# Threshold attention followed by a gMLP: half-batch loads shaped by GpSimd, and gMLP work two steps later

## The chip, the cores and the metric

One NeuronCore of a Trainium2 chip. The metric is device time in microseconds (us) of one execution. The kernel before took 701.15 us, the median of three runs (699.99 to 705.87). Engines are named as in the profile: PE is TensorE (PEld its weight loads), DVE VectorE, ACT ScalarE, POOL GpSimd, SP SyncE, whose queue (SPq) issues nearly all DMAs here. "Rounds" are repeated timings of a kernel beside the kernel before on the same chip.

## The reference, cut to what matters

Shapes: q, k, v are 8 batches x 8 heads x 576 x 64; the gMLP has 512 inputs and 1024 hidden columns.

```python
scores = scale * np.matmul(q, k.transpose(0, 1, 3, 2))
thresh = np.max(scores, axis=-1, keepdims=True) - tau          # tau = 0.02
scores = np.where(scores >= thresh, scores, -1e9)
attn = exp(scores - max); attn /= attn.sum(-1) + 1e-9
x = (attn @ v)  -> (B, S, H*D)
h = np.maximum(x @ w_in, 0);  u, v = h[..., :512], h[..., 512:]
v_n = (v - mean(v)) / np.sqrt(var(v) + 1e-6)                   # LayerNorm (LN)
v_s = w_spatial @ v_n + b_spatial
out = (u * v_s) @ w_out
```
(The middle lines are abridged.)

## The kernel before: the parts concerned

Thirty-two pairs of heads are walked as *slots*, each of five *steps* of query rows. A step makes scores on PE, their maxima on DVE (`negm`), exponentials on ACT (`e`), the thresholded product on DVE (`p`, "the mask"), and a transposing DMA (`pT`; `pTr` for the half-size fifth step). The scores of 64 key columns of each head are one product with `kd`, a small operand that Pool copies together. One or two filler products stand behind the scores: the transposes of the next pair's q and k (`qk_main`), the product with v (`pv`), or a piece of the gMLP (`moe_v`, `moe_u`, `moe_s`, `moe_o`).

```python
for slot in range(NPAIR + 5):
    i = slot if slot < NPAIR else None
    for c in range(5):
        fillers = []
        # ... qk_main(slot + 1, 0/1) at c = 0/1, qk_rem at c = 2; pv(slot - 1) at c = 3, 4
        if slot >= 5:
            b, ph = divmod(slot - 5, 4)
            fillers.append((moe_v, moe_u, moe_s, moe_o)[ph](b, c))
        step(i, c, fillers)
        if c == 3 and slot + 2 < NPAIR:
            load(slot + 2)          # q, k, v of one pair, q and k in runs of 256 B
```
When a pair's output is complete, it is transposed into `xT`, and a part of it moved by Pool:

```python
# end of pv, second head
nc.sync.dma_start_transpose(out=xts[b][:, hp, :]..., in_=xns[i]...)
nc.gpsimd.tensor_copy(out=xts[b][64:128, hp, 512:576], in_=xts[b][64:128, hp, 576:640])
```
Pool took its instructions in the order of this program.

Of the kernel before, what the change touches and what calls it, by code (L numbers as in the profile page):

```python
# [8 lines left out]
F32 = mybir.dt.float32  # L9
# [8 lines left out]
def kernel(  # L18
# [14 lines left out]

    nc = tc.nc
# [6 lines left out]
    P = 128  # L41
    const = ctx.enter_context(tc.tile_pool(name="const", bufs=1))
    ld = ctx.enter_context(tc.tile_pool(name="ld", bufs=2))
    qkT = ctx.enter_context(tc.tile_pool(name="qkT", bufs=2))
    ep = ctx.enter_context(tc.tile_pool(name="ep", bufs=3))
    ptp = ctx.enter_context(tc.tile_pool(name="ptp", bufs=10))
# [3 lines left out]
    xtp = ctx.enter_context(tc.tile_pool(name="xtp", bufs=3))  # L50
# [17 lines left out]
    pr_ring = [const.tile([P, 640], BF16, name=f"pr{i}") for i in range(2)]  # L68
    v_ring = [const.tile([P, 2, 6, D + 1], BF16, name=f"v{i}") for i in range(4)]
    vn_ring = [const.tile([P, 5, 512], BF16, name=f"vn{i}") for i in range(2)]  # L70
    kd_ring = [const.tile([P, P], F32, name=f"kd{i}") for i in range(2)]
    qd_ring = [const.tile([P, P], F32, name=f"qd{i}") for i in range(2)]
    for t in kd_ring + qd_ring:
        nc.gpsimd.memset(t, 0.0)
    for t in pr_ring:
        nc.gpsimd.memset(t[:, S:640], 0.0)
    for t in v_ring:
        nc.gpsimd.memset(t[:, :, :, D:D + 1], 1.0)
        nc.gpsimd.memset(t[64:128, 0, 4, :], 0.0)
        nc.gpsimd.memset(t[0:64, 1, 4, :], 0.0)  # L80
        nc.gpsimd.memset(t[64:128, 1, 5, :], 0.0)
# [7 lines left out]
    wsl = const.tile([P, 5, S], F32, name="wsl")  # L89
# [4 lines left out]


    loaded = {}

    def load(i):
        b, hp = divmod(i, HP)
        ts = []  # L100
        for nm, src in (("qn", q), ("kn", k)):
            t = ld.tile([P, 5, 2, D], F32, name=nm)
            for h in range(2):
                nc.sync.dma_start(  # L104
                    out=t[:, 0:4, h, :],
                    in_=src[b, 2 * hp + h, 0:512, :].rearrange("(p c) d -> p c d", c=4))
            nc.sync.dma_start(out=t[0:64, 4, :, :],  # L107
                              in_=src[b, 2 * hp:2 * hp + 2, 512:576, :].rearrange("h p d -> p h d"))
            ts.append(t.rearrange("p c h d -> p c (h d)"))
        t = ld.tile([P, 2, 5, D], F32, name="vl")  # L110
        s2 = v[b, 2 * hp:2 * hp + 2]
        nc.sync.dma_start(
            out=t[:, :, 0:4, :],
            in_=s2[:, 0:512, :].rearrange("h (p c) d -> p h c d", c=4))
        nc.sync.dma_start(out=t[0:64, :, 4, :],
                          in_=s2[:, 512:576, :].rearrange("h p d -> p h d"))
        nc.sync.dma_start(out=t[64:128, 1, 4, :], in_=s2[1, 512:576, :])
        ts.append(t)
        loaded[i] = ts
        vt = v_ring[i % 4]  # L120
        nc.gpsimd.tensor_copy(out=vt[:, :, 0:4, 0:D], in_=ts[2][:, :, 0:4, :])  # L121
        nc.gpsimd.tensor_copy(out=vt[0:64, 0, 4, 0:D], in_=ts[2][0:64, 0, 4, :])
        nc.gpsimd.tensor_copy(out=vt[0:64, 1, 5, 0:D], in_=ts[2][0:64, 1, 4, :])
        nc.gpsimd.tensor_copy(out=vt[64:128, 1, 4, 0:D], in_=ts[2][64:128, 1, 4, :])


    def load_weights():
        nc.gpsimd.dma_start(out=w_in, in_=moe_w_in.rearrange("(f p) n -> p f n", p=P))
        nc.gpsimd.dma_start(out=w_o, in_=moe_w_out.rearrange("(f p) n -> p f n", p=P))
        nc.sync.dma_start(out=wsl[:, 0:4, :],  # L130
                          in_=moe_w_spatial[0:512, :].rearrange("(p c) s -> p c s", c=4))
        nc.sync.dma_start(out=wsl[0:64, 4, :], in_=moe_w_spatial[512:576, :])
        brow = const.tile([1, S], F32, name="brow")
        nc.sync.dma_start(
            out=brow[0:1, 0:512].rearrange("o (c p) -> o c p", c=4),
            in_=moe_b_spatial[0:512].rearrange("(o p c) -> o c p", o=1, c=4))
        nc.sync.dma_start(out=brow[0:1, 512:576],
# [3 lines left out]
        for c in range(5):  # L141
            n = P if c < 4 else 64
            nc.gpsimd.tensor_copy(
                out=wsb[:n, c, 0:512].rearrange("p (sc sp) -> p sc sp", sc=4),
                in_=wsl[:n, c, 0:512].rearrange("p (sp sc) -> p sc sp", sc=4))
            nc.gpsimd.tensor_copy(out=wsb[:n, c, 512:576], in_=wsl[:n, c, 512:576])
        for c in range(5):
            nc.sync.dma_start_transpose(out=wsT[:, :, c * P:(c + 1) * P], in_=wsb[:, c, :])
# [15 lines left out]
    qts, kts, rems, pts, xns, xts = {}, {}, {}, {}, {}, {}  # L164

    def qk_main(i, which):
        src = loaded[i][which]
        dst = qkT.tile([P, 512], F32, name="qT" if which == 0 else "kT")
        (qts if which == 0 else kts)[i] = dst
        hold = {}  # L170

        def mm():
            t = ps_f.tile([P, 512], F32, name="f")
            hold["t"] = t
            for c in range(4):
                nc.tensor.transpose(out=t[:, c * P:(c + 1) * P], in_=src[:, c, :],  # L176
                                    identity=identf)

        def ev():
            nc.scalar.activation(out=dst, in_=hold["t"], func=ACT.Copy,  # L180
                                 scale=scale if which == 0 else 1.0)
        return mm, ev

    def qk_rem(i):
        hold = {}

        def mm():
            t = ps_f.tile([P, 512], F32, name="f")
            hold["t"] = t
            for w in range(2):  # L190
                nc.tensor.transpose(out=t[:, w * 64:w * 64 + 64],
                                    in_=loaded[i][w][0:64, 4, :],
                                    identity=identf[0:64, 0:64])

        def ev():
            rem = qkT.tile([P, P], F32, name="rem")
            rems[i] = rem
            nc.scalar.copy(out=rem, in_=hold["t"][:, 0:P])
            for lo in (0, 64):
                hs = slice(lo, lo + 64)  # L200
                nc.gpsimd.tensor_scalar(out=qd_ring[i % 2][hs, hs], in0=rem[hs, 0:64],
                                        scalar1=scale, scalar2=0.0, op0=ALU.mult, op1=ALU.add)
                nc.gpsimd.tensor_copy(out=kd_ring[i % 2][hs, hs], in_=rem[hs, 64:128])  # L203
        return mm, ev

    def pv(i, h):
# [4 lines left out]
        def mm():  # L211
            t = ps_f.tile([P, 512], F32, name="f")
            hold["t"] = t
            for c in range(5):
                for ki in range(5):
                    blk = ki if (c == 4 or h == 0 or ki == 4) else 5 + ki
                    vb = 5 if (c == 4 and h == 1 and ki == 4) else ki
                    nc.tensor.matmul(out=t[:, c * 65:c * 65 + 65], lhsT=pts[i, c][:, blk, :],  # L218
                                     rhs=vt[:, h, vb, :], start=(ki == 0), stop=(ki == 4))
# [17 lines left out]
        return mm, ev  # L237

    vns, us, gs = {}, {}, {}

    def moe_v(b, c):
# [9 lines left out]
        def ev():  # L251
            vrel = vr.tile([P, 512], F32, name="vrel")
            nc.scalar.activation(out=vrel, in_=hold["t"], func=ACT.Relu)  # L253
            st = small.tile([P, 6], F32, name="st")
            nc.vector.bn_stats(out=st, in_=vrel)  # L255
            mv = small.tile([P, 2], F32, name="mv")
            nc.vector.bn_aggr(out=mv, in_=st)
            rs = small.tile([P, 1], F32, name="rs")
            nc.gpsimd.tensor_scalar(out=rs, in0=mv[:, 1:2], scalar1=1e-6, scalar2=1.0,
                                    op0=ALU.add, op1=ALU.mult)  # L260
            nc.gpsimd.tensor_tensor(out=rs, in0=rs, in1=mhalf, op=ALU.pow)
            nm = small.tile([P, 1], F32, name="nm")
            nc.gpsimd.tensor_scalar(out=nm, in0=mv[:, 0:1], scalar1=rs, scalar2=-1.0,
                                    op0=ALU.mult, op1=ALU.mult)
            n = P if c < 4 else 64
            nc.gpsimd.tensor_scalar(out=vn_ring[b % 2][:n, c, :], in0=vrel[:n],  # L266
                                    scalar1=rs[:n], scalar2=nm[:n],
                                    op0=ALU.mult, op1=ALU.add)
        return mm, ev

    def cols(n):
        return (0, 512) if n == 0 else (512, 64)

    def moe_u(b, f):
# [17 lines left out]
        def ev():  # L292
# [3 lines left out]
            if f < 4:  # L296
# [5 lines left out]
        return mm, ev  # L302

    def moe_s(b, f):
# [28 lines left out]
        return mm, ev  # L333

    def moe_o(b, c):
# [10 lines left out]
        def ev():  # L346
            o = vr.tile([P, 512], F32, name="o")
            nc.scalar.copy(out=o[:n], in_=hold["t"][:n])
# [3 lines left out]
        return mm, ev  # L352


    pend_ev = []
    pend_mask = []

    def step(i, c, fillers):

        if i is not None:  # L360
            qT, kT = qts[i], kts[i]
            s = ps_s.tile([P, 1536], F32, name="s")
            A, Bh = slice(0, 64), slice(64, 128)
            if c < 4:
                cs = slice(c * P, (c + 1) * P)


                nc.tensor.matmul(out=s[:, 0:512], lhsT=qT[A, cs], rhs=kT[A, :],  # L368
                                 start=True, stop=True)
# [113 lines left out]
```

## Time and profile before

| | before |
|---|---|
| median | 701.15 us |
| busy: PE / DVE / ACT / POOL | 73 / 68 / 42 / 30% |
| PE waits for q's load | 52.0 us in 28 slots |
| PE waits for xT before moe_v | 41.2 us in 8 batches |
| first row maxima | 33.19 us after the start |

Busy shares alone say little here: no engine is full. The lines of the profile stand in the prediction, with their reading.

### The profile page before, as it was taken

Reading aid. Unit: us, or ns where it says so; the run is one execution under the profiler, and the core shown is the slowest. Engines: PE = TensorE matmul, PEld = TensorE weight load, DVE = VectorE, ACT = ScalarE, POOL = GpSimd, SP = SyncE. Lnnn points to the kernel's source line nnn. Section 1 sums busy time; section 2 is a strip of 40 time slices with the busy share of each in tenths; the row PEclk is TensorE's granted clock in tenths of the full one; section 3 lists DMA queues with packets and bytes.
Section 4 is the critical chain, followed back from the end, with each engine's and each line's share of the span. In section 5 each row is a group of like instructions: output and inputs, shape, how many; then the busy total and the mean of one; then the engine's idle time right before and its main releaser. Section 6 shows DMA issues by size and latency. Waiting matters only on the chain.

```text
span 704.7 us, 10528 instructions
## 1 busy us (share of the span) xinstructions
PE 517.9 (73%) x3712; PEld 265.5 (38%) x3712; DVE 479.0 (68%) x570; ACT 299.2 (42%) x506; POOL 209.1 (30%) x497
## 2 busy tenths in 40 slices
PE   2177775888856788578858888567896888588876
PEld 1034442444423444244424444234442444244432
DVE  0067776788837787487857888377864888578931
ACT  1044444364524544354443645245352554336332
POOL 5601112451214311344114511143112452145031
PEclk9977777899979999899988999899997999889999
DMA  6947877377956567468693779565575677838531
GB/s 169 145 101 134 147 134 155 54 141 141 179 125 115 114 121 172 102 121 139 127 197 62 144 139 182 122 110 116 107 176 112 113 141 140 195 64 139 97 103 67
DMA packets 297786, 90.94 MB, mean 129 GB/s; under 512 B 283718, under 2 KB 292422, under 8 KB 297606
## 3 DMA queue, kind: packets, MB, share of 16 engines
q1 hardware_dynamic: 296678, 88.71, 64.8%
q0 software_dynamic: 1056, 1.57, 1.4%
q8 instruction: 29, 0.48, 0.3%
q14 instruction: 23, 0.19, 0.1%
HBM read 33.31 MB, written 9.44 MB: 61 GB/s over the span
## 4 chain that ended last, share of the span: by engine, by line
PE 28%; DVE 22%; DMA 14%; SPq 11%; ACT 11%; issue 8%; POOL 5%; POOLq 0%; ACTq 0%; DVEq 0%
DVE negm L386 12%; PE s L368 10%; DMA qn<-in_q_dram 9%; ACT e L389 7%; DVE p L402 6%; SPq L104 5%; PE s L372 4%; DMA xT<-xn 3%; PE f L218 3%; PE f L176 3%; PE f L343 2%; PE f L282 2%; POOL vn L266 2%; SPq L406 2%; SPq L107 2%
## 5 line engine op out<-in xcount | busy, mean ns | idle before, releaser
L389 ACT ACTIVATE e<-s,negm 128x576 f32<-128x576 f32 x256 | 175.7, 738 | 284.0 <-DVE negm L386 284.0
L386 DVE TENSOR_REDUCE negm<-s 128x2 f32<-128x1152 f32 x128 | 172.8, 1350 | 114.2 <-PE s L372 113.6
L402 DVE SCALAR_TENSOR_TENSOR p<-e,ctau 128x1152 bf16<-128x1152 f32 x128 | 181.5, 1418 | 0.0
L368 PE MATMUL s<-kT,qT 64*128 64x512 f32 x256 | 163.3, 721 | 4.2 <-ACT e L389 3.8
L370 PE MATMUL s<-kT,qT 64*128 64x512 f32 x256 | 163.3, 721 | 0.0
L121 POOL CAST v<-vl 128x512 bf16<-128x512 f32 x32 | 19.8, 618 | 291.3 <-DMA vl<-in_v_dram 245.0
L372 PEld LDWEIGHTS s<-kd,qT 128*128 128x128 f32 x256 | 41.4, 203 | 133.2 <-issue 107.7
L372 PE MATMUL s<-kd,qT 128*128 128x128 f32 x256 | 67.4, 348 | 21.6 <-POOL kd L203 21.6
L248 PE MATMUL f<-w_in,xT 128*128 128x512 bf16 x160 | 48.8, 427 | 41.5 <-DMA xT<-xn 41.2
L255 DVE BATCH_NORM_STATS2 st<-vrel 128x6 f32<-128x512 f32 x40 | 27.7, 692 | 73.7 <-ACT vrel L253 73.5
L218 PE MATMUL f<-v,pT 128*128 128x65 bf16 x1280 | 51.1, 193 | 34.1 <-ACT vrel L253 12.9
L176 PE MATMUL f<-identf,qn 128*128 128x128 f32 x128 | 23.8, 317 | 59.0 <-DMA qn<-in_q_dram 52.0
L218 PEld LDWEIGHTS <-pT 128*128 128x128 bf16 x1280 | 49.6, 99 | 40.4 <-issue 34.3
L368 PEld LDWEIGHTS s<-kT,qT 64*128 64x128 f32 x256 | 42.9, 209 | 53.2 <-issue 36.9
L266 POOL TENSOR_SCALAR vn<-vrel,rs,nm 128x512 bf16<-128x512 f32 (+1 forms) x40 | 53.2, 1329 | 4.0
L253 ACT ACTIVATE vrel<-f 128x512 f32<-128x512 f32 x40 | 24.1, 602 | 46.4 <-PE f L248 43.3
L343 PE MATMUL f<-w_o,gT 128*128 128x512 bf16 (+1 forms) x160 | 41.4, 387 | 2.8 <-DVE xn L227 1.7
L370 PEld LDWEIGHTS s<-kT,qT 64*128 64x128 f32 x256 | 42.9, 209 | 0.0
L313 PE MATMUL f<-wsT,vn 128*128 128x512 bf16 x160 | 41.0, 390 | 2.3 <-POOL vn L266 1.4
L396 ACT ACTIVATE e<-s,negm 128x576 f32<-128x576 f32 x32 | 23.7, 741 | 40.6 <-DVE negm L393 40.6
L176 PEld LDWEIGHTS f<-identf,qn 128*128 128x128 f32 x128 | 15.9, 159 | 63.8 <-issue 63.8
L248 PEld LDWEIGHTS <-xT 128*128 128x128 bf16 x160 | 15.8, 108 | 59.1 <-DMA xT<-xn 45.5
(71 smaller groups left out, 633.0 us busy)
## 6 DMA issues: line engine op xcount, KB each, us to landing
qn<-in_q_dram SPq DMA_DIRECT2D x64, 128.0 KB, 2.9
kn<-in_k_dram SPq DMA_DIRECT2D x64, 128.0 KB, 2.8
vl<-in_v_dram SPq DMA_DIRECT2D x32, 256.0 KB, 3.0
out_dram<-o SPq DMA_DIRECT2D x32, 256.0 KB, 2.6
pT<-p SPq DMA_TRANSPOSE x128, 3.3
wsl<-in_moe_w_spatial_dram SPq DMA_DIRECT2D x1, 1152.0 KB, 6.1
qn<-in_q_dram SPq DMA_DIRECT2D x32, 32.0 KB, 2.5
kn<-in_k_dram SPq DMA_DIRECT2D x32, 32.0 KB, 2.4
```

What stands on the lines that cost most here:

```text
L176: nc.tensor.transpose(out=t[:, c * P:(c + 1) * P], in_=src[:, c, :], identity=identf)
L218: nc.tensor.matmul(out=t[:, c * 65:c * 65 + 65], lhsT=pts[i, c][:, blk, :], rhs=vt[:, h, vb, :], start=(ki == 0), stop=(ki == 4))
L248: nc.tensor.matmul(out=t, lhsT=xts[b][:, f, c * P:(c + 1) * P], rhs=w_in[:, f, 512:1024], start=(f == 0), stop=(f == 3))
L266: nc.gpsimd.tensor_scalar(out=vn_ring[b % 2][:n, c, :], in0=vrel[:n], scalar1=rs[:n], scalar2=nm[:n], op0=ALU.mult, op1=ALU.add)
L313: nc.tensor.matmul(out=t, lhsT=vn[:, c, f * P:(f + 1) * P], rhs=wsT[:, c, 0:512], start=(c == 0), stop=(c == 4))
L343: nc.tensor.matmul(out=t[:n], lhsT=gs[b][:, f, c * P:c * P + n], rhs=w_o[:, f, :], start=(f == 0), stop=(f == 3))
L368: nc.tensor.matmul(out=s[:, 0:512], lhsT=qT[A, cs], rhs=kT[A, :], start=True, stop=True)
L370: nc.tensor.matmul(out=s[:, 1024:1536], lhsT=qT[Bh, cs], rhs=kT[Bh, :], start=True, stop=True)
L372: nc.tensor.matmul(out=view(s, 512, [[448, 2], [1, 64]]), lhsT=qT[:, cs], rhs=kd_ring[i % 2], start=True, stop=True)
L386: nc.vector.tensor_reduce(out=nm, in_=both, axis=AX.X, op=ALU.max, negate=True)
L389: nc.scalar.activation(out=e[:, h, :], in_=both[:, h, :], func=ACT.Exp, bias=nm[:, h:h + 1])
L402: nc.vector.scalar_tensor_tensor(out=pt, in0=pe.rearrange("p h s -> p (h s)"), scalar=ctau, in1=pe.rearrange("p h s -> p (h s)"), op0=ALU. ...
```

## The change

Its intent: load two pairs at once in 1 KB runs, two slots ahead, so that PE never waits for q; let moe_v start two steps later (27 steps instead of 25), so that its xT has landed; make masks and transposes of the last step simpler; take LN's statistics from DVE to ACT; bring the weights in while slot 1 runs. The core of the diff:

```diff
+    def load_qk(i, n):                     # n = 2: both pairs of half a batch
+        ...
+            nc.sync.dma_start(
+                out=t[:, :, 0:4, :],
+                in_=src[:, 0:512, :].rearrange("h (p c) d -> p h (c d)", c=4))
+    def shape_qk(i):                       # Pool: head-interleaved copy for the transposes
+        ...
+            if w == 0:
+                nc.gpsimd.tensor_scalar(out=t, in0=src, scalar1=scale, ...)
+            else:
+                nc.gpsimd.tensor_copy(out=t, in_=src)
...
-            nc.vector.bn_stats(out=st, in_=vrel)
-            nc.vector.bn_aggr(out=mv, in_=st)
+            nc.scalar.activation(out=vrel, in_=hold["t"], func=ACT.Relu, accum_out=sm)
+            ...
+                nc.scalar.activation(out=sq, in_=vrel, func=ACT.Square, bias=nmean,
+                                     accum_out=ss)
...
-        for slot in range(NPAIR + 5):
+    LAG = 27
+        for g in range(20 * B + LAG):
+            slot, c = divmod(g, 5)
+            if c == 0 and i is not None:
+                if slot % 2 == 0 and slot + 2 < NPAIR:
+                    load_qk(slot + 2, 2)
+                    load_v(slot + 2)
+                if slot + 1 < NPAIR:
+                    shape_qk(slot + 1)
+                shape_v(slot)
+                if slot == 1:
+                    load_weights()
```
(The last batch has its own placement, with LN on DVE, uT evacuated by DVE and every other output copy on DVE; the last step's scores are four small products; its `pTr` is transposed in two halves. The lines are abridged, and `...` stands for what is left out.) The xT copy stays where it was, at the end of `pv`. In the program it now comes directly ahead of the next `shape_qk`.

## The prediction

> **What bounds the kernel now.** I read the page, then the list of waits, the timeline of some slots, and the gaps in TensorE's timeline. A *slot* is one pair of heads, five *steps* of 128 query rows (the fifth is half size). In each step TensorE makes the scores and one or two filler products, DVE takes row maxima (`negm`), ACT the exponentials, DVE masks (`p`), and the DMA transposes.
>
> ```profile
> PE 517.9 (73%) x3712; PEld 265.5 (38%) x3712; DVE 479.0 (68%) x570; ACT 299.2 (42%) x506; POOL 209.1 (30%) x497
> ...
> PEclk9977777899979999899988999899997999889999
> ...
> L386 DVE TENSOR_REDUCE negm<-s 128x2 f32<-128x1152 f32 x128 | 172.8, 1350 | 114.2 <-PE s L372 113.6
> ...
> L402 DVE SCALAR_TENSOR_TENSOR p<-e,ctau 128x1152 bf16<-128x1152 f32 x128 | 181.5, 1418 | 0.0
> ```
>
> No engine is full. DVE is next to TensorE, and a step costs it 1.35 + 1.42 = 2.77 us. What stretches a slot is in the waits:
>
> ```profile
> ACT e L389 <- DVE negm L386: 284.0, 128, 25.8
> ...
> PE f L176 <- DMA qn<-in_q_dram: 52.0, 28, 5.0
> ...
> PE f L248 <- DMA xT<-xn: 41.2, 8, 6.3
> ```
>
> The first is only ACT's spare time. The second is the start of nearly every slot: the next pair's q arrives late because its load is issued one step ahead. The third comes once per batch: the first gMLP product (moe_v) follows directly on the last head's output, whose transpose has not landed. The timeline shows both, with TensorE's cold clock after the longer one (a score pass of 1.22 us, otherwise 0.69):
>
> ```profile
> 309.11 0.63 PE L176 MATMUL f<-identf,qn 128*128 128x128 f32 x4 [1.20 <-DMA qn<-in_q_dram]
> ...
> 326.66 0.63 PE L176 MATMUL f<-identf,qn 128*128 128x128 f32 x4 [1.89 <-DMA qn<-in_q_dram]
> ...
> 366.19 1.35 SPq L406 DMA_TRANSPOSE pT<-p  x1
> ...
> 367.63 1.24 SPq L232 DMA_TRANSPOSE xT<-xn  x1
> ...
> 370.27 0.61 PE L248 MATMUL f<-w_in,xT 128*128 128x512 bf16 x1 [5.55 <-DMA xT<-xn]
> 370.28 0.24 POOL L235 COPY xT<-xT 64x64 bf16<-64x64 bf16 x1 [2.22 <-DMA xT<-xn]
> ...
> 370.81 1.22 PE L368 MATMUL s<-kT,qT 64*128 64x512 f32 x1
> ```
>
> I mark a slot by T, the start of its q transposes. T runs from 144.03 to 636.81 over six batches: 82.1 us a batch, 20.5 a slot; a moe_u slot is 17.55 (309.11 to 326.66), and the slot with moe_v has 27. Before that, the start: scores are ready at 11 us, but their correction operand `kd` stands on Pool behind the preparation of the weights:
>
> ```profile
> 8.51 0.26 ACT L198 COPY rem<-f 128x128 f32<-128x128 f32 x1
> ...
> 31.28 0.23 POOL L201 TENSOR_SCALAR qd<-rem 64x64 f32<-64x64 f32 x1
> ...
> 32.35 0.80 PE L372 MATMUL s<-kd,qT 128*128 128x128 f32 x2 [21.61 <-POOL kd L203]
> ```
>
> **What the Trainium skill says.** *TensorE: Matmul & The Clock Gate*, Part 1: an idle window of about 3.4 us halves the clock, and a similar busy time restores it. Agrees: each gap of 3.4 us or more in the before trace is followed by about 4 us of slow passes; several gaps of only 1.9 to 2.3 us are too. *GPSIMD Engine Reference*, Specifications: Pool shares its SBUF interfaces with VectorE and contends with DVE instructions with two SBUF inputs. Agrees; the mask is one, and a 0.26 us Pool operation that starts inside it ends with it:
>
> ```profile
> 319.78 1.41 DVE L402 SCALAR_TENSOR_TENSOR p<-e,ctau 128x1152 bf16<-128x1152 f32 x1
> ...
> 319.84 1.48 POOL L263 TENSOR_SCALAR nm<-mv,rs 128x1 f32<-128x1 f32 x1
> ```
>
> *DMA: Bandwidth & Descriptors*, Specifications: runs of 512 B and more are needed for line rate. Here q lands 128 KB in 256 B runs in 2.9 us and v 256 KB in 1 KB runs in 3.0 us: long runs carry more, but what is waited for is latency. *ScalarE: Activation LUTs*, What ACT_TABLE_LOAD costs: 280 ns + 0.833 ns per element with a pointer bias. The exponentials agree (0.74 us for 576).
>
> **The change part by part.**
>
> Loads. Two pairs are fetched together, two slots ahead: the wait for q's DMA (52 us, plus SP's issue time before it) goes. But Pool must now bring q and k into shape at the top of the slot in which TensorE transposes them. By the order of Pool's instructions in the changed build, each slot's q shaping stands directly *behind* the small xT copy (L235 before), which waits for the xT transpose of the step just ended. A new chain replaces the load: xn, SP, xT DMA, Pool copy, Pool shaping, q transpose. Shaping 640 elements I estimate at 0.92 us: Pool's unblocked tensor_scalar takes 0.77 for 512 and 0.19 for one element.
>
> The slot, walked from T = 0 in a moe_u slot. q transposes 0.5, filler 0.9 and scores 1.55 end at 2.95. From there DVE has: max 1.36, mask 1.41, max, mask (8.5), a gap of 0.35 for TensorE, max, mask (11.6), xn 0.7, short max 0.74, mask 1.41, xn 0.7: 15.15. SP issues the mask's transpose first (1.3 us from 14.5, to 15.8), xT lands 2.6 later (18.45), copy 0.3 (18.75), q shaping with hand-over 1.0: the next T is at 19.75. Before it was 17.55: 2.2 us lost. TensorE has finished the next slot's first scores at 14.9 and idles 4.85 us, longer than before's 1.2 to 1.9.
>
> The other three slots of a batch. With moe_s the output products are the first filler and xn comes before the mask, so xT starts at 14.85: 18.75 in all. The slot after it has two gT products left on DVE: 20.4. The slot in which moe_v starts has its LN work on Pool (rs, pow, nm, vn of three blocks, some 2.1 us each, stopped during masks) ahead of the xT copy: the walk gives 22.25; the next, with two more squares on ACT, 20.5. Sum 18.75 + 20.4 + 22.25 + 20.5 = 81.9 a batch with a warm clock. This already contains the gains: xT is now two steps ahead of moe_v (41 us of waiting off), bn_stats and bn_aggr leave DVE (35 us of 479, seven eighths of it), a Square of about 0.71 us (estimate from the ScalarE page) goes to ACT, which has room at 42%. So what is gained in the moe_v slots (27 to 22) is given back in the others: 81.9 against 82.1.
>
> The clock. Four gaps of 2.7 to 7 us per batch instead of one of 5.5 to 6 and some of 2. A cold start delays the filler and first scores by about 1.7 us (a score group ran 2.65 us instead of 1.5, the filler 1.41 instead of 1.03, cut off after 4 us). Three or four per batch: 5 to 6 us, up to 88 a batch. Over the 6.75 batches with gMLP: -1 to +40 us.
>
> Start. kd no longer waits for the weights: first maxima at about 14 instead of 33.19 us, 19 gained. But load_weights now runs in slot 1 through three buffers of the exponentials' ring, and SP holds its loads and transposes in turn: three loads of some 4 us, five blocks of casts at 1.3, five wsT issues at 1.3 to 2, then 4.6 us for the bias; SP frees the pending `pTr` at about 55. I find the T of slot 2 at 67, against 66.56 before. Slots 2 to 4 have the new chain as well (18 instead of 17): in all +5.
>
> The rest. Fifth step as four small products (about 1.3 us, as now), kd first: nothing. The split pTr adds one SP issue of 1.25 us a slot, not on the chain. Tail: two more steps, but LN partly on DVE and output copies on two engines: -2.
>
> Sum: 701 + 5 - 2 - 1 = 703 warm; 701 + 5 - 2 + 40 = 744 with every slot cold.
>
> **Rivals.** (1) The loads were the bound and shaping is hidden: slots near 18, DVE's 14.35 us plus 3 to 4. For it: DVE is contiguous in my walk and only the chain keeps the slot at 20; against it: Pool is in order and the copy's wait stands ahead. It would make 640 to 670. (2) DVE or ACT becomes the bound: DVE's total of about 455 us plus start and tail says no. (3) The weights' stall in slot 1 is much shorter, 40 instead of 67: 10 to 20 us off, 685 to 695. (4) Pool shaping slowed by masks or by strided reads, 1.5 to 2 us rather than 0.9: 30 us more, 735 to 770.
>
> **Range and chances.** The sum spans 703 to 744. The cold case agrees better with the gaps before, but the change is plainly tuned (a lag of 27, a last batch of its own), which makes me suspect that my serial walk overstates a hand-over somewhere; so I put the time at 718, below the middle. Range 680 to 750: rival 3 at the low end, the cold sum at the high. Faster by over 2% (under 687) needs rival 1 or 3: 0.22. Within 2%: 0.30. Slower: 0.48.
>
> **What would show it.** TensorE's q transposes should wait for Pool's qn (instead of DMA), 3 to 5 us in nearly every slot, and Pool's xT copy for the xT DMA just before; the wait of moe_v for xT should be gone; T to T about 20 in moe_u slots; score passes of 1.22 us at most slot starts, mean clock at or below 0.91; DVE near 455 us; the first maxima at 14 us and a hole between 30 and 60. If q transposes wait less than 1.5 us a slot, my chain is wrong and rival 1 holds.

## The result, and the profile after

The changed kernel took 755.5 us (median of 4 runs, 749.93 to 757.43), the kernel before 701.85 us beside it (4 runs, 699.99 to 705.87): ratio 1.074, 95% interval 1.068 to 1.081. A ratio is the mean time of one kernel's runs over that of the other's in the same rounds, so not quite the ratio of the medians quoted. The change was slower by 7%, and the time lies outside the predicted range. All outputs are right.

Busy times and the granted clock of the changed kernel (from the page; each digit is a fortieth of the span, in tenths of full speed):

```profile
PE 528.8 (71%) x3840; PEld 278.6 (37%) x3840; DVE 460.4 (62%) x516; ACT 324.6 (43%) x605; POOL 210.2 (28%) x427
PEclk9755987888988999988988999888998789989998
```
DVE fell from 479.0 to 460.4 us, as intended. PE's busy time grew by 11 us although its large products are the same (3840 instructions against 3712, since the fifth step's scores are now four small products): it ran colder, with a mean granted clock of 0.86 against 0.912. The same 128 q transposes, for one, took 33.2 us instead of 23.8.

The list of waits of the changed kernel (engine, who is waited for: us in total, times, longest):

```profile
POOL xT L261 <- DMA xT<-xn: 234.2, 25, 13.1
...
PEld f L208 <- POOL qn L142: 172.3, 30, 8.1
...
PE f L208 <- POOL qn L142: 147.8, 30, 7.3
```
The 52 us of waiting for q's DMA became 147.8 us of waiting for Pool to shape q, 4.9 us on average in 30 slots. The first line tells what Pool was doing: standing at the small copy until the xT transpose landed. The stall that the lag of 27 was meant for is gone: moe_v waited for xT once, 2.7 us, against 41.2 us in 8 batches.

One such slot start, from the timeline (start, duration, engine, instruction; in brackets the idle time before and who ended it):

```profile
427.28 0.49 DVE L253 TENSOR_TENSOR xn<-f,r 128x320 bf16<-128x320 f32 x1
...
428.60 1.25 SPq L258 DMA_TRANSPOSE xT<-xn  x1
...
431.31 0.23 POOL L261 COPY xT<-xT 64x64 bf16<-64x64 bf16 x1 [5.41 <-DMA xT<-xn]
...
431.63 0.72 POOL L142 TENSOR_SCALAR qn<-ql 128x640 f32<-128x640 f32 x1
...
432.41 1.12 PE L208 MATMUL f<-identf,qn 128*128 128x128 f32 x4 [4.29 <-POOL qn L142]
...
433.32 1.91 PE L324 MATMUL f<-xT,w_in 128*128 128x512 bf16 x4
```
Read it downwards: the output `xn` ends at 427.77, SP gets to its transpose 0.8 us later, Pool's copy starts at 431.31 when it has landed, only then does Pool shape q, for whose load it does not have to wait, and PE starts at 432.41. That is 4.64 us from `xn` to PE. The last line is the clock: the product of four takes 1.91 us where a warm one takes 1.04.

PE's q transposes at the start of four consecutive slots in the changed kernel:

```profile
237.40 1.11 PE L208 MATMUL f<-identf,qn 128*128 128x128 f32 x4 [7.27 <-POOL qn L142]
...
259.26 1.11 PE L208 MATMUL f<-identf,qn 128*128 128x128 f32 x4 [4.24 <-POOL qn L142]
...
279.37 0.65 PE L208 MATMUL f<-identf,qn 128*128 128x128 f32 x4 [2.52 <-POOL qn L142]
...
299.19 1.11 PE L208 MATMUL f<-identf,qn 128*128 128x128 f32 x4 [5.28 <-POOL qn L142]
```
Slots of 21.9, 20.1 and 19.8 us; the fourth ends at 322.52 (23.3 us): 85.1 us for the batch, where the kernel before needs 82.1 by the prediction's reading and 83.1 on average from pair 6 to pair 31.

Where the 43.3 us between the two profiled spans (704.7 to 748.0) arose follows from three marks on PE, the start of the q transposes T of pair 6 and of pair 31, and the end: pair 6 at 130.29 instead of 117.44 (+12.9, the start), pair 31 at 671.00 instead of 636.81 (34.2 late, so +21.3 in the loop), the end 43.3 late (+9.1 in the tail). The marks split the span, so they add up by construction. They do not cover everything: the profiled execution of the kernel before was a slow one of its kind (706.51 us) and that of the changed kernel its fastest (749.93), while the medians are 53.7 us apart. Where the other 10 us arise, these two traces do not tell.

The start of the changed kernel, where the weights come in (timeline):

```profile
13.53 1.36 DVE L460 TENSOR_REDUCE negm<-s 128x2 f32<-128x1152 f32 x1 [12.63 <-PE s L415]
...
34.23 0.54 SPq L170 DMA_DIRECT2D e<-in_moe_w_spatial_dram  x1
41.80 1.07 POOL L178 CAST wsb<-e 128x512 bf16<-128x512 f32 x1 [14.18 <-DMA e<-in_moe_w_spatial_dram]
...
44.28 1.37 ACT L468 ACTIVATE e<-s,negm 128x576 f32<-128x576 f32 x2 [16.02 <-POOL wsb L181]
...
63.99 1.25 SPq L443 DMA_TRANSPOSE pTr<-pr  x1
```
The maxima come at 13.5 us instead of 33.2, but then a piece of w_spatial, held in one of the three buffers of the exponentials, stops ACT for 16 us, SP with the transposes of `wsb` and the bias lets `pTr` go only at 64, and the 20 us gained are lost and more.

In the tail, LN's blocks of the last batch follow one another on DVE and Pool, hand by hand (timeline of the changed kernel; the last of five blocks, and the next product of u):

```profile
726.83 0.69 DVE L287 BATCH_NORM_STATS2 st<-vrel 128x6 f32<-128x512 f32 x1
727.55 0.18 DVE L289 BATCH_NORM_AGGREGATE mv<-st 128x2 f32<-128x6 f32 x1
727.77 0.15 DVE L290 TENSOR_SCALAR rs<-mv 128x1 f32<-128x1 f32 x1
728.00 0.55 POOL L292 TENSOR_TENSOR rs<-rs,mhalf 128x1 f32<-128x1 f32 x1 [1.67 <-DVE rs L290]
728.59 0.54 DVE L293 TENSOR_SCALAR vn<-vrel,mv,rs 64x512 bf16<-64x512 f32 x1 [0.66 <-POOL rs L292]
729.77 3.23 PE L324 MATMUL f<-xT,w_in 128*128 128x512 bf16 x8 [5.50 <-DVE uT L339]
```
A block takes 2.2 us, and DVE waits 0.66 us for Pool's one-element power within each. That alone is no loss: in the kernel before, a block took 2.15 us on Pool. But DVE now also evacuates u, behind all five blocks, and so PE waits 5.50 us for `uT`. From the block of moe_v products at 716.76 to the first moe_s product (733.79) it is 17.0 us, in the kernel before 10.6 (678.3 to 688.9).

### The profile page after: what moved, and what is told of

It is laid out like the page before. It is cut to its first block, busy times and chain, and to the rows that moved or that the text cites. A ratio compares the mean times of both kernels' runs of the same rounds, so it can differ in the third digit from the quotient of the medians.

```text
span 748.0 us, 10560 instructions
## 1 busy us (share of the span) xinstructions
PE 528.8 (71%) x3840; PEld 278.6 (37%) x3840; DVE 460.4 (62%) x516; ACT 324.6 (43%) x605; POOL 210.2 (28%) x427
## 4 chain that ended last, share of the span: by engine, by line
PE 31%; issue 24%; POOL 17%; DVE 12%; DMA 7%; ACT 7%; SPq 1%; POOLq 0%; ACTq 0%; DVEq 0%
PE s L415 11%; PE f L208 6%; DVE p L434 5%; DVE negm L460 4%; POOL rs L309 4%; DMA xT<-xn 4%; PE f L275 3%; POOL vn L311 3%; ACT e L468 3%; POOL qn L142 3%; PE s L418 3%; ACT sq L305 3%; PE f L388 3%; PE f L324 2%; POOL nm L310 2%
## 5 line engine op out<-in xcount | busy, mean ns | idle before, releaser
L460 DVE TENSOR_REDUCE negm<-s 128x2 f32<-128x1152 f32 (+1 forms) x160 | 197.3, 1233 | 218.2 <-PE s L415 216.6
L415 PE MATMUL s<-qkT 64*128 64x512 f32 (+1 forms) x768 | 202.9, 621 | 1.3 <-ACT e L468 1.0
L208 PE MATMUL f<-identf,qn 128*128 128x128 f32 x128 | 33.2, 409 | 147.8 <-POOL qn L142 147.8
L212 ACT COPY qkT<-f 128x512 f32<-128x512 f32 x64 | 37.5, 586 | 227.8 <-PE f L208 221.5
L418 PE MATMUL s<-kd,qkT 128*128 128x128 f32 x256 | 61.5, 327 | 26.3 <-ACT e L468 23.7
L415 PEld LDWEIGHTS s<-qkT 64*128 64x128 f32 (+1 forms) x768 | 59.2, 184 | 32.1 <-issue 10.2
L418 PEld LDWEIGHTS s<-kd,qkT 128*128 128x128 f32 x256 | 52.4, 226 | 45.6 <-ACT e L468 23.5
L324 PE MATMUL f<-xT,w_in 128*128 128x512 bf16 x128 | 39.5, 440 | 14.2 <-ACT vrel L297 7.2
L305 ACT ACTIVATE sq<-vrel,nmean 128x512 bf16<-128x512 f32 x35 | 25.1, 721 | 32.7 <-POOL nmean L299 32.7
L253 DVE TENSOR_TENSOR xn<-f,r 128x320 bf16<-128x320 f32 x64 | 31.4, 491 | 2.2
L309 POOL TENSOR_TENSOR rs<-rs,mhalf 128x1 f32<-128x1 f32 x35 | 31.1, 887 | 2.9
```

The source lines that it names most:

```text
L208: nc.tensor.transpose(out=t[:, c * P:(c + 1) * P], in_=nat[i][which][:, c, :], identity=identf)
L305: nc.scalar.activation(out=sq, in_=vrel, func=ACT.Square, bias=nmean, accum_out=ss)
L309: nc.gpsimd.tensor_tensor(out=rs, in0=rs, in1=mhalf, op=ALU.pow)
L324: nc.tensor.matmul(out=t, lhsT=w_in[:, m, f * P:(f + 1) * P], rhs=xts[b][:, m, 0:512], start=(m == 0), stop=(m == 3))
L415: return nc.tensor.matmul(out=out, lhsT=qk[hs, 0, m], rhs=qk[hs, 1, lo:lo + n], start=True, stop=True)
L418: nc.tensor.matmul(out=view(s, 512, [[448, 2], [1, 64]]), lhsT=qk[:, 0, c * P:(c + 1) * P], rhs=kd_ring[i % 2], start=True, stop=True)
```

## The experiments

Thirteen kernels in four sets, each in three rounds. "Theory A" and "Rival R" change their meaning from set to set; the texts say it. All of the first set start from the changed kernel.

| run | starts from | median us | ratio to before (95%) |
|---|---|---|---|
| changed kernel | | 755.5 | 1.074 (1.068 to 1.081) |
| a1_late_copy | changed | 653.5 | 0.927 (0.922 to 0.932) |
| a2_warm | changed | 721.9 | 1.026 (1.019 to 1.033) |
| a3_weights | changed | 731.2 | 1.036 (1.029 to 1.043) |
| a4_tail | changed | 748.0 | 1.063 (1.056 to 1.069) |
| a5_all | a1 + a3 + a4 | 631.0 | 0.900 (0.896 to 0.903) |
| a6_bn | a5_all | 621.2 | 0.881 (0.876 to 0.887) |
| a7_shape | a5_all | 610.2 | 0.867 (0.862 to 0.873) |
| a8_both | a6 + a7 | 612.5 | 0.870 (0.867 to 0.874) |
| b1_lag | before | 647.7 | 0.923 (0.918 to 0.928) |
| b2_early | before | 648.4 | 0.923 (0.919 to 0.927) |
| b3_both | b1 + b2 | 634.4 | 0.904 (0.900 to 0.907) |
| b4_pool | b3 | 802.6 | 1.140 (1.133 to 1.146) |
| b5_pool | b3 | 621.1 | 0.882 (0.879 to 0.886) |

### a1_late_copy: Pool's xT copy behind the shaping

```diff
-                nc.gpsimd.tensor_copy(out=xts[b][64:128, hp, 512:576], ...)   # end of pv
+                fixups.append((b, hp))
...
             if c == 0 and i is not None:
                 ...shape_qk(slot + 1); shape_v(slot)
+            if c == 0:
+                fix()                     # the same copies, now after the shaping
```

> The changed kernel with one thing moved: Pool's small xT copy stands behind the slot's q, k and v shaping instead of ahead of it. Theory A (the chain xn, xT DMA, Pool copy, q shaping sets each slot): the wait of q transposes for Pool (148 us) falls under 40 us, slots go from 21.6 to 15 to 17 us, the whole to 600 to 640 us. Rival 1 (Pool's shaping work itself or the larger loads set the slot): the wait stays and the time stays above 720 us. Rival 2 (DVE or ACT is the bound anyway): the wait goes, the time stays above 690 us.

Measured: 653.5 us, 102 us less than the changed kernel. In a normal slot Pool now stands at the copy with nothing behind it that is urgent (timeline of a1_late_copy):

```profile
318.91 0.49 DVE L253 TENSOR_TENSOR xn<-f,r 128x320 bf16<-128x320 f32 x1
319.43 1.55 SPq L258 DMA_TRANSPOSE xT<-xn  x1
...
320.61 0.66 PE L208 MATMUL f<-identf,qn 128*128 128x128 f32 x4
...
323.70 0.24 POOL L268 COPY xT<-xT 64x64 bf16<-64x64 bf16 x1 [8.77 <-DMA xT<-xn]
...
336.73 0.65 PE L208 MATMUL f<-identf,qn 128*128 128x128 f32 x4
```
PE starts 3 us *before* the copy, without a wait, and this slot is 16.1 us long (18.0 on average from pair 6 to pair 31, 15 to 17 expected). The list of waits of a1_late_copy shows what remains:

```profile
PE f L208 <- POOL qn L142: 53.6, 8, 7.3
```
Once a batch instead of 30 times: in the slot after moe_v begins, LN's Pool work stands ahead of the shaping. So the chain, not the loads and not the shaping itself, cost the loop its time. The run came out 13 us above the expected 600 to 640; those 8 waits, 53.6 us, are longer than supposed (under 40 us).

### a2_warm: PE kept busy in the gap

```diff
+            if which == 0 and i >= 4:
+                for _ in range(10 if i % 4 == 1 else 16):     # results overwritten, never read
+                    nc.tensor.matmul(out=t, lhsT=w_in[:, 0, 0:P], rhs=w_in[:, 0, 0:512], ...)
```

> The changed kernel with 16 (one slot in four: 10) unused bf16 products of 512 columns on TensorE ahead of the q transposes, about 0.22 us each, so that its gap at the slot's start is filled and the clock stays warm; the chain is untouched. If the cold clock after the gap costs 1.1 to 1.7 us a slot: 30 to 48 us less, 707 to 725 us, and mean clock above 0.95. If the gap alone is the cost: same time within 1%, 748 to 763 us.

Measured: 721.9 us, 33.6 us less, with a clock of 0.94 (above 0.95 expected). PE still waits for qn in 30 slots (63.7 us in all, the unused products fill the rest), and most of the slow passes after the wait are gone. Over the 28 slots concerned that is 1.2 us a slot; by the marks of the two traces, pair 6 to pair 31 takes 518.0 us instead of 540.7, 0.9 a slot. The clock is therefore a consequence of the wait, worth a quarter (marks) to a third (medians) of what a1 gained by taking the wait away; the two are not to be added.

### a3_weights: the weights' work spread over slots 2 to 7

```diff
-                if slot == 1: load_weights()
+                if slot == 1: weights_load()          # DMAs only, w_spatial in a tile of its own
+            if c == 1 and 2 <= slot <= 6: weights_block(slot - 2)   # casts + one transpose
+            if c == 1 and slot == 7: weights_bias()
```

> The changed kernel with the spatial weights in a tile of their own, one block of 128 rows shaped and transposed per slot in slots 2 to 6 and the bias in slot 7, instead of all in slot 1 through the exponentials' ring. If slot 1's hole (q transposes of slots 1 and 2 lie 50.5 us apart) comes from the ring and SP's order: the hole falls to 18 to 22 us and the time by 25 to 32 us, to 723 to 731 us. If it comes from the DMA traffic of the weights: under 12 us off.

Measured: 731.2 us, 24 us less. T of slot 2 moved from 76.93 to 55.47 us, 21.5 us, so nearly all of the gain lies in the start. The hole itself, from T of slot 1 to T of slot 2, fell from 50.5 to 28.7 us, not to the expected 18 to 22.

### a4_tail: the last batch placed as the others of the kernel before

The LN statistics again feed four Pool operations in a row instead of going to and fro, and uT and output copies go to ACT.

```diff
-                nc.vector.tensor_scalar(out=dst, in0=vrel[:n], scalar1=mv[:n, 0:1], scalar2=rs[:n], ...)
+                nc.gpsimd.tensor_scalar(out=nm, in0=mv[:, 0:1], scalar1=rs, scalar2=-1.0, ...)
+                nc.gpsimd.tensor_scalar(out=dst, in0=vrel[:n], scalar1=rs[:n], scalar2=nm[:n], ...)
-        return ("dve" if b == B - 1 else "act"), mm, ev
+        return "act", mm, ev
```

> The changed kernel with the last batch's gMLP placed as in the kernel before: LN scale and shift on Pool, u evacuated by ACT, all outputs by ACT. If the last batch's own placement costs (its LN blocks follow each other on DVE at 2.2 us and u waits behind them): 5 to 8 us less, 747 to 751 us. If the longer tail comes from the two extra steps: same or slower, 755 to 760 us.

Measured: 748.0 us, 7.5 us less by the medians, with intervals that just touch. The traces agree in kind: from pair 31 to the end it is 71.7 us instead of 77.0, and from the moe_v block to moe_s 10.5 instead of 17.0, as in the kernel before. So the special tail costs some 5 of the 9.1 us. The two extra steps cost most of the rest: with the lag alone (b1, below) the same stretch is 70.9 us against 67.9 in the kernel before.

### b1_lag, b2_early, b3_both: two parts of the change alone, in the kernel before

b1 takes only the lag of 27, b2 only earlier loads, of the same old form; b3 both.

```diff
 b1  -                if slot >= 5:
     -                    b, ph = divmod(slot - 5, 4)
     +                n = 5 * slot + c - 27
     +                if 0 <= n < 20 * B:
     +                    b, r = divmod(n, 20)      # job r // 5, piece r % 5
 b2  -                if c == 3 and slot + 2 < NPAIR:
     +                if c == 0 and slot + 2 < NPAIR:
                          load(slot + 2)
```

> The kernel before with one part of the change alone: gMLP jobs 27 steps behind instead of 25, so that moe_v starts two steps after the last head's output. Theory A (what the first four runs left standing: the change's other parts are sound, its loss is Pool's order, the slot-1 weights and the tail): the wait of moe_v for xT (41 us, 5.5 a batch) goes, and with it one cold stretch of 1.2 to 2 us a batch: 8 times some 5.5 to 7, less two more steps at the end (2 to 4): 650 to 665 us. Rival R: the stall only moves to the next bound (DVE's work piled up in that slot, or q's DMA wait growing from 1.9 to 4): 690 to 702 us, ratio over 0.98.

> The kernel before with its loads issued at the first step of a slot instead of the fourth, nothing else (same 256 B runs, no shaping). Theory A: q's wait (52 us in 28 slots) goes nearly whole, 1 to 1.9 us a slot: 650 to 670 us. It would show that an earlier issue alone gives what the half-batch loads were for. Rival R: the issue of ten loads on SP in front of the last pTr delays the output products, or the buffers of two pairs are not yet free at that step, and the wait turns up there: 690 to 705 us.

> The kernel before with both: lag of 27 and loads at the first step. Theory A: the two gains are in different slots' waits and add: 600 to 625 us, faster than the changed kernel with Pool's order mended (653). Rival R: they do not add, since DVE with its bn_stats (479 us busy plus start 33 and tail 10) is next: 630 to 650 us.

Measured: 647.7, 648.4 and 634.4 us, that is 55, 54 and 68 us less than the kernel before. The first two agree with Theory A (b1 a little better, b2 just below its range). Together they do not add (their sum is 109), and b3 lies in Rival R's range. In part the gains overlap: the earlier loads of b2, besides taking q's wait from 52.0 to 5.0 us, also cut the wait for xT from 41.2 to 27.3. In part a new wait has come. The list of waits of b3_both:

```profile
POOL v L121 <- DMA vl<-in_v_dram: 228.8, 31, 12.5
...
PE s L372 <- POOL kd L203: 42.2, 13, 20.2
```
Both old waits are gone (one of 5.1 us for q is left, in the start). The new one: the cast of v follows its load in Pool's order, Pool stands in it until v lands, and the correction operand `kd` of the scores stands behind. 20 us of the 42.2 are in the start and were there before (21.6). It is the same fault as in the changed kernel, a waiting instruction in front of an urgent one on Pool. Rival R's reason, DVE (76% busy here), is not excluded: no run of this set took work off DVE.

### a5_all: the three mends together

> The changed kernel with the three mends at once (Pool's xT copy behind the shaping, weights spread over six slots, the last batch placed as before). Single effects were -102, -24 and -7.5 us. Theory A: they add, as they lie in different stretches: 615 to 630 us. Rival R: the start's hole hid part of Pool's chain, and they overlap: 635 to 650 us.

Measured: 631.0 us, on the border of the two: 124.5 us less than the changed kernel where the single effects add to 133.8. Mostly they add.

### b4_pool and b5_pool: Pool's order mended in the kernel before

b4 moves the cast of v to the last step of the slot that uses it, and spreads the weights' casts.

```diff
 b4  +                if c == 4 and slot < NPAIR:
     +                    vcast(slot)
 b5  +                if c == 4 and slot + 1 < NPAIR:
     +                    vcast(slot + 1)
```

> The kernel before with lag 27 and loads at the first step (634.4 us), and besides it the casts of v at the last step of the slot that uses them instead of directly at the load, and Pool's work on w_spatial spread over slots 2 to 7: nothing that waits for a DMA stands ahead of kd on Pool any more. Theory A (kd's 42 us of waiting, 20 in the start and 22 later, are Pool's order): most of it goes, 595 to 610 us. Rival R: DVE's 479 us and its gaps take over: 615 to 630 us.

Measured: 802.6 us, a miss by 200 us and my own mistake. The waits of SP's queue in b4_pool say it in one line:

```profile
SPq L113 <- POOL v L128: 216.8, 30, 11.1
```
There are two buffers for v's load. The load of pair s+2, issued at the first step of slot s, needs the buffer that pair s still holds until its cast, four steps later. SP waits in that load and all mask transposes stand behind: DVE's masks, which in the kernel before never waited for a transpose, waited 172.8 us for pT to free their buffers. b5 casts one slot earlier, so that the buffer is free in time.

> The previous build of this idea fell (802.6 us), and its trace says why: the cast of v came after the load that needs its buffer, so SP stood in that load with the transposes behind it. Here the same idea with the cast one slot earlier (v of the next pair at the last step of this slot), so that the buffer is free when the load is issued; weights' Pool work spread as before. Theory A (kd's wait of 42 us in the 634.4 us kernel was Pool standing at v's cast and at the weights): 595 to 612 us; then the loads in single pairs with 256 B runs, unshaped, do as well as the change's. Rival R (the unshaped loads are worse by themselves): 618 to 634 us.

Measured: 621.1 us. The wait for kd is gone (0.0 us in front of that product), so Theory A had the mechanism, but it gained only 13 us: Rival R's range. Not all of the wait was on the path; what bounds b5 now was not tested.

### a6_bn, a7_shape, a8_both: what is left in the mended changed kernel

a6 takes LN's statistics back to bn_stats on DVE for all batches (`if b == B - 1:` becomes `if True:`). a7 shapes one step earlier, ahead of LN's work:

```diff
-                if slot + 1 < NPAIR:
-                    shape_qk(slot + 1)      # first step of a slot
+                if slot == 0:
+                    shape_qk(1)
+            if c == 4 and slot + 2 < NPAIR:
+                shape_qk(slot + 2)          # last step of the slot before
```

> The mended changed kernel (the previous run: 631.0 us) with the LayerNorm of every batch by bn_stats and bn_aggr on DVE, as in the kernel before, instead of sums on ACT: this measures that part of the change alone, in a kernel where DVE is nearly contiguous. Theory A (DVE is now the bound in the moe_v slots): 35 blocks times 0.87 us come back to DVE, in two slots a batch that already end with DVE: up to 20 to 30 us slower, 645 to 660. Rival R (those slots end with the chain of Pool for LN and shaping, not with DVE; ACT's sums cost two more Pool steps and 0.7 + 0.4 us of ACT a block, so the chain gets shorter): 620 to 633, the same or faster.

> The mended changed kernel (631.0 us) with the shaping of q and k one step earlier (at the last step of the slot ahead of the one that uses them, in front of that step's LN work). Theory A (the 53 us of TensorE waiting for Pool's qn that are left, one of 7 us a batch, are the LN chain ahead of the shaping): wait under 10 us, 585 to 605 us. Rival R: Pool then waits for the loads issued in the same slot, or DVE becomes the bound at once: 615 to 631 us.

> The mended changed kernel with the last two mends together: shaping a step earlier (which alone gave 610.2 us) and LayerNorm by bn_stats on DVE (which alone gave 621.2; without either 631.0). Theory A (the two act on the same chain of Pool work in the moe_v slots, so they overlap, but the ACT sums still cost more than they free): 600 to 608 us. Rival R (they are the same gain counted twice, and with bn_stats DVE is the bound): 610 to 616 us.

Measured: 621.2, 610.2 and 612.5 us against a5's 631.0. a6: Theory A fell, Rival R holds. To give DVE 28 us of work back (460.4 to 488.7 us busy) made the kernel 10 us *faster*. The reason is in the cost of the ACT sums (groups of instructions of a5_all: count, busy us, mean ns, then idle time before them and whose end it was):

```profile
L312 ACT ACTIVATE sq<-vrel,nmean 128x512 bf16<-128x512 f32 x35 | 25.1, 722 | 32.2 <-POOL nmean L306 32.2
...
L304 ACT ACTIVATION_READ_ACCUMULATOR vrel<-f 128x1 f32 x35 | 7.3, 208 | 0.0
...
L314 POOL TENSOR_SCALAR rs<-ss 128x1 f32<-128x1 f32 x35 | 6.7, 190 | 48.7 <-ACT sq L312 48.1
```
ACT waits for Pool's mean, Pool for ACT's squares, and in that slot the shaping stands behind them. Those 8 waits for qn were 53.2 us in a5_all and are 20.9 in a6_bn.

a7: 20.8 us less and the fastest kernel of all (0.867). It misses the expected 585 to 605, since eight waits for qn of 31.9 us in all are left (under 10 expected). a8: Rival R; with the shaping ahead of LN, bn_stats gain nothing more (0.870 against 0.867, overlapping intervals). The waits for qn are down to 7.2 us there, but DVE is at 488.0 us, 80% of the span, against 459.2 in a7. So bn_stats helped a6 by shortening LN's chain in front of the shaping; once the shaping is out of its way, the shorter chain and the fuller DVE balance. That DVE is what takes the gain back is my reading of these two numbers, not shown by a run of its own. a8 and b5 ran in the same set: the changed kernel, well placed, beats the kernel before, well placed, by 1.4% (0.870 / 0.882; the intervals do not overlap). Which of the remaining differences (1 KB loads, merged keys, fewer Pool instructions) brings this was not separated.

## Why the prediction was wrong

- **The chain** (xn, SP, xT, Pool copy, shaping, q transposes) was right in kind and length: 4.6 us predicted from the end of xn to PE, 4.64 measured in the slot shown. PE's waits were 2.5 to 7.3 us from pair 6 on, 4.9 on average (3 to 5 predicted for nearly every slot). a1 showed that the chain is the cause. Most other signs came true too: first maxima at 13.5 us, moe_v's wait gone, mean clock 0.86.
- **The slots**: walked 81.9 us a batch warm and up to 88 cold; measured 85.1 in the batch shown, 86.5 on average from pair 6 to pair 31 (540.7 us over 25 slots; 83.1 before). The cold case nearly held: a cold start cost 0.9 to 1.2 us a slot (a2), below the 1.7 estimated. The loop as a whole gave +21.3 us, inside the -1 to +40.
- **The failed step** is the last one: "the change is plainly tuned ... which makes me suspect that my serial walk overstates a hand-over somewhere; so I put the time at 718, below the middle." No hand-over of the chain was overstated (4.64 us against 4.6), and the loop took more than the warm walk. The walk's cold end, 744, "agrees better with the gaps before" by its own words. That a kernel looks tuned is no measurement, and it outweighed one. (The direction was right: slower had the highest chance, 0.48.) The range ended at 750, just above the cold sum; the profiled execution lies at its edge (749.93), the median 755.5 outside, and where those last us arise stays open.
- **Two terms of the sum**, start and tail, were wrong besides (the next two points), by 19 us together.
- **The start** was mis-sized: +5 predicted, +12.9 measured. (The parts that the prediction gives for it, 0.4 us and three slots of 1 us, add to 3.4, not to 5.) T of slot 2 was put at 67 and came at 76.93. I took three loads of some 4 us; the first took 7.6 us from its issue to its cast (34.23 to 41.80) and was issued late, behind SP's transposes.
- **The tail** was wrong in sign: -2 predicted, +9.1 measured. I had counted the engines that share the work, and not that u's evacuation on DVE would stand behind all of LN (PE waits 5.50 us for it); the two extra steps, which the prediction named without a figure, cost 3.0 us in b1.
- **Luck**: the cold sum, 744, is 43 us above 701, and the two traces are 43.3 us apart. That is chance: start and tail were 19 us too small together, the cold loop term (+40) 19 us too large.
- **Shaping** took 0.72 us where it ran undisturbed, not 0.92. **DVE** 460.4 us, about 455 predicted.
- **Rival 1** (the loads were the bound, shaping is hidden, 640 to 670) is what a1 made true: 653.5 us, 18.0 us a slot, once the copy was out of the way. The condition against it, as told, held. **Rival 2** fell: no engine was the bound. **Rival 3** fell: the stall of the weights was longer, not shorter. **Rival 4** named the right time, 735 to 770, for a wrong reason: q's shaping averaged 0.74 us.
- **Where the expected gain went**: it existed. Lag and early loads alone bring 68 us in the kernel before (b3); the order of one 0.23 us copy on Pool took 102 us.

## What to carry to other kernels

Before moving work to a lightly used engine, ask what the instruction just ahead of it waits for: here Pool worked in program order, and a copy of 0.23 us that waited for a DMA held up shaping whose data were already there. Place what waits behind what is urgent, and check the same for the queue that issues the DMAs, where a load that waits for its buffer stops every transpose behind it. When a step-by-step sum stands against an impression of the kernel, keep the sum, and test single parts of a large change alone: two edits of a few lines gave 68 us in the kernel before.

## What the Trainium skill lacked or had wrong

- *ScalarE: Activation LUTs*, What it computes, says that an ACTIVATE can give an accumulator output, but not what that costs: each was followed by an ACTIVATION_READ_ACCUMULATOR on ACT of its own, 0.19 to 0.21 us on average, 70 of them in the changed kernel.
- *DMA: Bandwidth & Descriptors*, Specifications, asks for 512 B and more for line rate. The page's fit of time against size is for DMAs that GpSimd issues; it has none for loads that SP issues, as here: q's 512 KB in 1 KB runs took 4.4 us from issue to landing, 128 KB in 256 B runs had taken 2.9. Lead time was what mattered (b2: earlier issue alone, 54 us).
- *TensorE: Matmul & The Clock Gate*, Part 1, puts the cold clock after an idle window of about 3.4 us. In the changed kernel every gap of 4.2 us and more in the loop was followed by slow passes, but shorter ones differ: the 2.52 us gap shown was not, while two others of 2.5 us (from 449.26 and 624.88) were.
- *GPSIMD Engine Reference* does not tell what an operation on one element per partition costs: the power took 0.55 us where it ran undisturbed, a `tensor_scalar` 0.19.
